# Transposing the attention weights by a DMA through memory instead of on TensorE in a top-k attention and MLP kernel

## The chip, the core and the metric

The kernel runs on one core of a Trainium2 chip. The core has five engines that each work through their own queue of instructions in order: TensorE (PE; its weight loads are listed as PEld), VectorE (DVE), ScalarE (ACT), GpSimd (POOL) and SyncE (SP), which here only issues DMAs. The metric is the device time of one execution in microseconds (us), the median of some runs. All times come from these runs or from one profiled execution.

## The reference

The first half is attention with the 32 largest scores of each row kept; the second is a two-layer network on its output. Cut to what is computed:

```python
# q, k, v: (8, 8, 576, 64) float32
scores = matmul(q, k.transpose(0, 1, 3, 2)) / sqrt(64)
kth = np.partition(scores, -32, axis=-1)[..., -32:-31]
scores = np.where(scores >= kth, scores, -1e9)
attn = np.exp(scores - scores.max(-1, keepdims=True))
attn = attn / (attn.sum(-1, keepdims=True) + 1e-9)
x = matmul(attn, v) -> (4608, 512)               # heads side by side
h = x @ w_in                                      # (512, 2048)
g = np.where(h >= 1, h, np.where(h <= -1, 0, (h + 1) ** 2 / 4))
out = g @ w_out                                   # (2048, 512)
```

Everything is float32.

## The kernel before

**Steps.** The attention is cut into 144 steps. A step takes 128 queries and two heads (or, for the last 64 rows of each head, two pairs of heads at once), so that its scores are two tiles of 128 x 576. In step m, `weights` (line 271) works on VectorE: four rounds of "the eight largest" (MAX8, line 283) and "strike them out" (line 292) on the pairwise maximum of a row's halves, then a correction from the pairwise minimum (lines 297 to 304), which gives the 32nd largest. ScalarE takes the exponentials (line 287) beside that. Line 312 keeps those whose score reaches the 32nd and sums them; lines 317 and 318 form the reciprocal of the sum; in most steps GpSimd multiplies the weights by it (line 325).

**Around a step.** `scores` (line 244) makes the scores two steps ahead on TensorE, and ScalarE copies them out of PSUM (line 261). `transpose_w` (line 333) follows a step later: eight TensorE transposes of 128 x 128 (line 344), and a ninth (line 352) for the two 64-column remainders, each into PSUM, and three ScalarE copies to SBUF (lines 345, 353). `values` (line 356) multiplies the transposed weights with v (line 364) and copies the result into `xT` (line 377), the input of the network. Once a tile of `xT` is complete, `mlp` (line 389) hands out units of work: `hidden` (four matmuls on line 394, the activation in pieces on ScalarE, lines 398 and 412, and on GpSimd, lines 413 to 415) and `final` (line 422, with one copy on line 426 and one store on line 428).

**Early and late.** In the first steps the weights of the network are also converted in 64 pieces by ScalarE, VectorE and GpSimd (`convert_piece`, line 110). While that goes on a step is "early", and its division is not done by GpSimd: ScalarE multiplies the identity by the reciprocals (line 322), and TensorE multiplies the weights by this diagonal, which transposes and divides in one (lines 342 and 349). The flag is `st["by_tensor"]`. 12 steps are of this kind and 132 are late ones. In late steps each piece of the network's weights is loaded once more and inspected by ScalarE (`inspect_piece`, line 138), one a step, until all 64 are through.

**The order of the work** is written out by hand for PE, DVE, ACT and POOL. The main loop goes through the steps; each has seven slots, and in each slot the next parts of `weights` are issued, then the other work due in that slot, and then `advance` adds units of the network by a rough count of times, as much as an equal share of the remaining work. In a late step before the change: values of step m - 2 and scores of step m + 2 at the start, the parts of `weights` as `[1, 2, 2, 2, 0, 0, 0]` (the last of the seven parts is the division), the transposes of step m - 1 in slot 2. As an engine works in order, what is issued behind a waiting instruction waits too. SP issues all DMAs in one queue.

The second call, `run(inner, False)`, is only executed if a test on the data asks for it; it is not executed with these inputs.

Of the kernel before, what the change touches and what calls it, by code (L numbers as in the profile page):

```python
# [10 lines left out]
F32 = mybir.dt.float32  # L11
U32 = mybir.dt.uint32
# [11 lines left out]
def kernel(  # L24
# [23 lines left out]
    SH = S // 2  # L48
    NK = DM // P
# [45 lines left out]
    def load(pool, i):  # L95
        if i < n_pieces and i not in loaded:
            if room and i < 28:
                loaded[i] = room[i % 8]
            else:
                loaded[i] = pool.tile([P, 2 * WC], U32, name="raw", bufs=3)  # L100
            nc.sync.dma_start(out=loaded[i], in_=pieces_of_weights[i][1].bitcast(U32))

    def words_of(pool, i):
        load(pool, i)
        words = loaded.pop(i).rearrange("p (n t) -> p n t", t=2)
        return words[:, :, 0], words[:, :, 1]
# [31 lines left out]
    def inspect_piece(pool, i):  # L138

        _, hi = words_of(pool, i)  # L140
        for x in range(2):
            sign = pool.tile([P, WC], F32, name="sign", bufs=3)
            nc.scalar.activation(sign, hi.bitcast(F32), AF.Sign, bias=tiny[:, x:x + 1],
                                 accum_out=signs[:, x, i:i + 1])


    def run(ctx, paired):
        xtp = ctx.enter_context(tc.tile_pool(name="xtp", bufs=3))
        stage = ctx.enter_context(tc.tile_pool(name="stage", bufs=2))
        att = ctx.enter_context(tc.tile_pool(name="att", bufs=2))  # L150
        ps = ctx.enter_context(tc.tile_pool(name="ps", bufs=1, space=PSUM))
# [119 lines left out]
        def weights(st, after):  # L271
# [47 lines left out]
            if st["by_tensor"]:  # L319
                st["rz"] = diag = att.tile([P, 2, P], F32, name="diag", bufs=1)  # L320
                for i in range(2):
                    nc.scalar.activation(diag[:, i, :], ident, AF.Copy, scale=rz[:, i:i + 1])
            else:
                for i in range(2):
                    nc.gpsimd.tensor_scalar(e[:, i, :], e[:, i, :], rz[:, i:i + 1], 1.0, ALU.mult, ALU.mult)  # L325
# [7 lines left out]
        def transpose_w(st):  # L333
            w = st["e"]
            st["wT"] = wT = att.tile([P, 2, NT, P], F32, name="wT", bufs=1)
            st["wTt"] = wTt = att.tile([P, P], F32, name="wTt", bufs=1)
            for i in range(2):
                pt = ps.tile([P, NT, P], F32, name="pw", tag="a", bufs=4)
                for c in range(NT):
                    w_in_place = w[:, i, main(i)][:, c * P:(c + 1) * P]  # L340
                    if st["by_tensor"]:
                        nc.tensor.matmul(pt[:, c, :], w_in_place, st["rz"][:, i, :], start=True, stop=True)
                    else:
                        nc.tensor.transpose(pt[:, c, :], w_in_place, ident)  # L344
                nc.scalar.copy(wT[:, i], pt)  # L345
            pt = ps.tile([P, P], F32, name="pwt", tag="a", bufs=4)
            if st["by_tensor"]:
                for i in range(2):
                    nc.tensor.matmul(pt[i * TL:(i + 1) * TL, :], w[:, i, tail(i)], st["rz"][:, i, :],
                                     start=True, stop=True)  # L350
            else:
                nc.tensor.transpose(pt, w.rearrange("p i n -> p (i n)")[:, SM:SM + P], ident)
            nc.scalar.copy(wTt, pt)


        def values(st):
            t, hp, v_in, v_tl = st["t"], st["hp"], st["keys"]["v"], st["keys"]["v_tl"]
            wT, wTt = st["wT"], st["wTt"]
            po = ps.tile([P, P], F32, name="po", tag="ph", bufs=3)
            if t < NT:  # L360
                for c in range(NT + 1):
                    for j in range(2):
                        h = 2 * hp + j
                        nc.tensor.matmul(po[j * D:(j + 1) * D], v_in[:, h, c, :] if c < NT else v_tl[0][:, h, :],  # L364
                                         wT[:, j, c, :] if c < NT else wTt, start=(c == 0), stop=(c == NT))
            else:
                for i in range(2):
                    cols = slice(i * TL, (i + 1) * TL)
                    for c in range(NT + 1):
                        for j in range(2):  # L370
                            h = 2 * (hp + i) + j
                            nc.tensor.matmul(po[j * D:(j + 1) * D, cols], v_in[:, h, c, :] if c < NT else v_tl[1][:, h, :],
                                             wT[:, i, c, j * TL:(j + 1) * TL] if c < NT else wTt[:, j * TL:(j + 1) * TL],
                                             start=(c == 0), stop=(c == NT))
            xT, col = st["xT"]
            if t < NT:
                nc.scalar.copy(xT[:, hp, col:col + P], po)  # L377
            else:
                nc.scalar.copy(xT[:, hp:hp + 2, col:col + TL], po.rearrange("p (i n) -> p i n", i=2))
# [88 lines left out]
        mlp_pool = ctx.enter_context(tc.tile_pool(name="mlp", bufs=1))  # L468
        pending = deque()
# [5 lines left out]
        def convert(time):  # L475

            nonlocal converted, begun
            while begun < min(converted + (2 if paired else 1), n_pieces):
                pipe.append(convert_piece(mlp_pool, begun, not paired))
                next(pipe[-1])  # L480
                begun += 1
# [3 lines left out]
            for i in range(begun, converted + 6):  # L485
                if i < converted + (2 if paired else 3) + (begun > converted) or room and i < 28:
                    load(mlp_pool, i)

        def inspect():
            nonlocal inspected  # L490
            room.clear()
            if paired and inspected < n_pieces:
                inspect_piece(mlp_pool, inspected)
                inspected += 1
                load(mlp_pool, inspected)
# [3 lines left out]
        pe_time, dve_time, done, scored, usable = 9.0, 12.0, {}, {}, {0: 0.0}  # L499
# [70 lines left out]
        for i in range(2):  # L570
            load(mlp_pool, i)
        next(first)
        for i in range(2, 8 if room else 3):
            load(mlp_pool, i)
# [12 lines left out]
        def values_until(m):  # L587
            nonlocal valued, pe_time
            while valued < min(m, n):
                pe_time = max(pe_time, transposed + 1.8) + 1.25  # L590
# [13 lines left out]

        for m in range(n + 2):
            early = converted < n_pieces
            coming = min((r + 2 - m for r in ready if r + 2 > m), default=1)
            if not early:
                values_until(m - 1)
                begin_at(m + 2)  # L610
            share = min((total - spent) / (n + 2 - m), sum(work[0] for work in pending) / coming)
            top_k, parts = None, [0] * SLOTS
            if m < n:
                top_k = weights(state[m], state[m + 1] if m + 1 < n else None)
                parts = [1] * SLOTS if early else [1, 2, 2, 2, 0, 0, 0]
# [5 lines left out]
            for slot in range(SLOTS):  # L621
# [6 lines left out]
                elif slot == 3:  # L628
                    inspect()
                if slot == 1 + (not early) and 1 <= m <= n:  # L630
                    pe_time = max(pe_time, done[m - 1] + 2.0) + 1.0
                    transpose_w(state[m - 1])
                    transposed = pe_time
                if slot == 2 and m == n and paired:
                    judge(ps, att)
                if slot == 2 and early:
# [3 lines left out]
                if slot == 4 and early:  # L640
                    begin_at(m + 2)
                if slot == (5 if early else 4):
# [63 lines left out]
```

## Time and profile before

| | |
|---|---|
| median of 3 runs | 1746.18 us (1745.42 to 1746.61) |
| the profiled execution | 1746.35 us |
| its span, first to last instruction | 1744.5 us |
| granted TensorE clock, mean | 0.982 of full speed |
| late steps | 132, from about 190 to 1700 us |
| DMA, mean over the span | 43 GB/s |

A group of instructions in the profile is one line, engine and operation, written out<-in with the names of the tiles; it shows the number of instructions, their total busy time and mean length, and the idle time of the engine just before them with what ended it. A table of windows gives each engine's busy time in stretches of the span. A chain of waits follows the work that ended last back to the start. Lengths of matmuls are those of a pipeline: successive ones overlap.

### The profile page before, as it was taken

The numbers are of one execution on the slowest core, as the hardware profiler recorded it, in microseconds if no ns is written. First come the engines' busy times: TensorE is split into PE (matmuls) and PEld (weight loads), VectorE is DVE, ScalarE is ACT, GpSimd is POOL, SyncE is SP. The second block draws the span as 40 slices with busy tenths as digits, with TensorE's granted clock in tenths as the row PEclk, the third lists the DMA queues.
The fourth block names the chain that finished last, engine by engine and source line by source line (L and its number), as shares of the span: only waits on it lengthen the run. The fifth ranks groups of instructions, "written<-read, shape, count | busy, mean of one in ns | idle before, by whom it ended". The sixth has DMA issues, their size and how long they took to land.

```text
span 1744.5 us, 33535 instructions
## 1 busy us (share of the span) xinstructions
PE 1639.4 (94%) x10665; PEld 1151.5 (66%) x10665; DVE 1537.0 (88%) x4875; ACT 1083.2 (62%) x2942; POOL 946.9 (54%) x1668
## 2 busy tenths in 40 slices
PE   5588989999999999999999999999999999999998
PEld 4476575667766757476756767567667666666665
DVE  7999979888899999999987999999997998899752
ACT  6688575676667857576655647556555555466452
POOL 5689183665544817264646645436365554555550
PEclk7799999999999999999999999999999999999999
DMA  8333112111121112111200101000010000000000
GB/s 253 116 98 97 46 30 65 44 43 41 42 63 52 44 49 65 46 49 41 62 13 22 25 22 44 17 24 17 23 39 19 19 10 14 13 7 7 7 7 15
DMA packets 116668, 74.63 MB, mean 43 GB/s; under 512 B 87296, under 2 KB 95488, under 8 KB 116480
## 3 DMA queue, kind: packets, MB, share of 16 engines
q1 hardware_dynamic: 116480, 72.37, 14.5%
q8 instruction: 87, 1.43, 0.3%
q14 instruction: 101, 0.83, 0.2%
HBM read 62.91 MB, written 9.44 MB: 41 GB/s over the span
## 4 chain that ended last, share of the span: by engine, by line
PE 65%; DVE 14%; POOL 11%; ACT 6%; issue 3%; DMA 0%; POOLq 0%; DVEq 0%; SPq 0%; ACTq 0%
PE py L422 25%; PE ph L394 18%; PE sp L258 7%; PE po L364 7%; PE pw L344 5%; DVE tops L283 4%; DVE more L292 3%; POOL g L415 3%; POOL r L414 3%; DVE e L312 3%; POOL e L325 2%; POOL r L413 2%; ACT s L261 1%; DVE seconds L300 1%; ACT r L398 1%
## 5 line engine op out<-in xcount | busy, mean ns | idle before, releaser
L394 PE MATMUL ph<-xT,w_in 128*128 128x128 f32 (+1 forms) x3200 | 558.0, 326 | 14.4 <-ACT g L412 13.2
L422 PE MATMUL py<-w_out,g 128*128 128x512 f32 x1152 | 530.9, 600 | 2.0 <-ACT y L426 2.0
L394 PEld LDWEIGHTS ph<-xT,w_in 128*128 128x128 f32 x3200 | 472.3, 192 | 87.9 <-ACT g L412 26.0
L325 POOL TENSOR_SCALAR e<-e,rz 128x576 f32<-128x576 f32 x264 | 195.0, 750 | 520.2 <-DVE rz L318 488.8
L283 DVE MAX8 tops<-more 128x8 f32<-128x288 f32 x1152 | 465.4, 445 | 0.0
L292 DVE MATCH_REPLACE8 more<-tops,more 128x288 f32<-128x288 f32 x864 | 375.6, 442 | 0.0
L422 PEld LDWEIGHTS py<-w_out,g 128*128 128x128 f32 x1152 | 205.2, 190 | 224.1 <-issue 215.8
L312 DVE SCALAR_TENSOR_TENSOR e<-s,kth,e 128x576 f32<-128x576 f32 x288 | 245.7, 881 | 116.6 <-ACT e L287 116.3
L398 ACT ACTIVATE r<-ph,half 128x128 f32<-128x128 f32 (+1 forms) x400 | 166.5, 416 | 216.8 <-POOL g L415 156.7
L415 POOL TENSOR_TENSOR g<-r,g 128x128 f32<-128x128 f32 (+1 forms) x384 | 255.9, 666 | 30.2
L413 POOL TENSOR_SCALAR r<-r 128x128 f32<-128x128 f32 (+1 forms) x368 | 173.2, 471 | 132.0 <-ACT r L398 131.7
L414 POOL TENSOR_TENSOR r<-r 128x128 f32<-128x128 f32 (+1 forms) x368 | 213.9, 581 | 30.7
L261 ACT ACTIVATE s<-sp 128x288 f32<-128x288 f32 x576 | 195.2, 421 | 56.8 <-PE sp L258 36.8
L287 ACT ACTIVATE e<-s,nmax 128x576 f32<-128x576 f32 x288 | 213.4, 770 | 7.7
L364 PEld LDWEIGHTS po<-wT,v_in 128*64 128x64 f32 x2048 | 111.8, 137 | 87.9 <-issue 53.2
L258 PE MATMUL sp<-kT,qT 64*128 64x288 f32 x1024 | 163.9, 437 | 4.2 <-ACT kT L218 2.3
L364 PE MATMUL po<-wT,v_in 128*64 128x128 f32 x2048 | 145.5, 280 | 18.7 <-ACT g L412 11.3
L345 ACT COPY wT<-pw 128x512 f32<-128x512 f32 x288 | 154.0, 589 | 13.1 <-PE pw L344 10.6
L344 PEld LDWEIGHTS pw<-ident,e 128*128 128x128 f32 x1056 | 122.2, 142 | 60.0 <-issue 24.4
L344 PE MATMUL pw<-ident,e 128*128 128x128 f32 x1056 | 141.0, 276 | 16.2 <-ACT s L261 10.4
L377 ACT COPY xT<-po 128x128 f32<-128x128 f32 x128 | 34.1, 266 | 195.8 <-PE po L364 195.5
L412 ACT ACTIVATE g<-ph,minus 128x128 f32<-128x128 f32 (+1 forms) x368 | 153.6, 417 | 0.0
(91 smaller groups left out, 1595.1 us busy)
## 6 DMA issues: line engine op xcount, KB each, us to landing
raw<-in_moe_w_out_dram SPq DMA_DIRECT2D x64, 256.0 KB, 2.6
raw<-in_moe_w_in_dram SPq DMA_DIRECT2D x36, 256.0 KB, 2.7
k_in<-in_k_dram SPq DMA_DIRECT2D x64, 128.0 KB, 2.9
q_in<-in_q_dram SPq DMA_DIRECT2D x32, 256.0 KB, 3.1
v_in<-in_v_dram SPq DMA_DIRECT2D x8, 1024.0 KB, 5.8
out_dram<-y SPq DMA_DIRECT2D x32, 256.0 KB, 2.3
kT<-in_moe_w_in_dram SPq DMA_DIRECT2D x16, 256.0 KB, 4.0
v_in<-in_moe_w_in_dram SPq DMA_DIRECT2D x12, 256.0 KB, 4.5
```

The lines of the kernel that those rows point to most:

```text
L258: nc.tensor.matmul(o[:, a0 - c0:a1 - c0], qT[d, g, :], kT[d, g, k0:k0 + a1 - a0], start=True, stop=True)
L283: nc.vector.max(out=tops[:, i, r:r + 8], in_=src[:, i, :])
L287: nc.scalar.activation(e[:, i, :], s[:, i, :], AF.Exp, bias=nmax[:, i:i + 1])
L292: nc.vector.match_replace(out=rest[:, i, :], in_to_replace=tops[:, i, r:r + 8], in_values=src[:, i, :], imm_value=LOWEST)
L312: nc.vector.scalar_tensor_tensor(out=e[:, i, :], in0=s[:, i, :], scalar=last[:, i:i + 1], in1=e[:, i, :], op0=ALU.is_ge, op1=ALU.mult, acc ...
L325: nc.gpsimd.tensor_scalar(e[:, i, :], e[:, i, :], rz[:, i:i + 1], 1.0, ALU.mult, ALU.mult)
L344: nc.tensor.transpose(pt[:, c, :], w_in_place, ident)
L364: nc.tensor.matmul(po[j * D:(j + 1) * D], v_in[:, h, c, :] if c < NT else v_tl[0][:, h, :], wT[:, j, c, :] if c < NT else wTt, start=(c == ...
L394: nc.tensor.matmul(ph, w_in[:, kk, f * P:(f + 1) * P], xT[:, kk, c0:c1], start=(kk == 0), stop=(kk == NK - 1))
L414: nc.gpsimd.tensor_tensor(out=r, in0=r, in1=r, op=ALU.mult)
L415: nc.gpsimd.tensor_tensor(out=g, in0=r, in1=g, op=ALU.add)
L422: nc.tensor.matmul(py, gs[f][:, i * P:(i + 1) * P], w_out[:, f, :], start=(f == 0), stop=(f == NF - 1))
```

## The change

Late steps no longer transpose on TensorE. A new function, `move_w`, splits each 32-bit weight into its two 16-bit halves with ScalarE copies (the low halves of a row side by side, then the high ones), stores them to a tile in memory, and loads that tile with a transposing DMA, which works on 16-bit elements. In the loaded tile the two halves of a weight lie side by side again, so that it can be read as float32. The tile has nine blocks of 128 (`BLOCKS`), the middle one holding both remainders, in the place of the former `wT` and `wTt`. `transpose_w` is left for early steps, in the diagonal form alone.

The order of a late step changes too. The division is not issued in slot 3 but as the last part of the step, behind the network's work of slots 4 to 6. `move_w` stands in slot 1. Scores of step m + 2 and values of step m - 2 go from the start of a step to slot 4. The rough count of times has the transposed weights ready 13.0 us after the step's end instead of 1.8 us after the transposes.

The buffers of the conversion are now in a pool of their own (`words`), which is closed once the conversion is over; its room is used for a new pool (`late`) with two buffers for the transposed weights, one for the halves, and two instead of three for the pieces under inspection. The first late step is a step of passage in which neither is done.

```diff
+        dram = ctx.enter_context(tc.tile_pool(name="dram", bufs=3, space=bass.MemoryType.DRAM))
...
         def transpose_w(st):
             w = st["e"]
-            st["wT"] = wT = att.tile([P, 2, NT, P], F32, name="wT", bufs=1)
-            st["wTt"] = wTt = att.tile([P, P], F32, name="wTt", bufs=1)
+            st["wT"] = wT = words.tile([P, BLOCKS, P], F32, name="wT")
...
+        def move_w(st):
+            st["wT"] = wT = late.tile([P, BLOCKS, P], F32, name="wT", bufs=2)
+            halves = late.tile([P, 2, 2 * S], U16, name="halves")
+            for i in range(2):
+                nc.scalar.copy(halves[:, :, i * S:(i + 1) * S], st["e"][:, i, :].bitcast(U16).rearrange("p (k t) -> p t k", t=2))
+            rows = dram.tile([P, 2, 2 * S], U16, name="rows")
+            nc.sync.dma_start(out=rows, in_=halves)
+            nc.sync.dma_start_transpose(wT.bitcast(U16), rows.rearrange("p t k -> (p t) k"))
+
+        def block(i, c):
+            return i * (NT + 1) + c if c < NT else NT
...
-                pe_time = max(pe_time, transposed + 1.8) + 1.25
+                pe_time = max(pe_time, ready_at[valued]) + 1.25
                 values(state[valued])
...
+        first_late = None
         for m in range(n + 2):
             early = converted < n_pieces
...
-            if not early:
-                values_until(m - 1)
-                begin_at(m + 2)
+            if not early and first_late is None:
+                first_late = m
+            elif not early and late is None:
+                conversion.close()
+                late = ctx.enter_context(tc.tile_pool(name="late", bufs=1))
...
-                parts = [1] * SLOTS if early else [1, 2, 2, 2, 0, 0, 0]
+                parts = [1] * SLOTS if early else [1, 2, 2, 1, 0, 0, 0]
...
-                elif slot == 3:
+                elif slot == 3 and late is not None:
                     inspect()
-                if slot == 1 + (not early) and 1 <= m <= n:
-                    pe_time = max(pe_time, done[m - 1] + 2.0) + 1.0
-                    transpose_w(state[m - 1])
-                    transposed = pe_time
+                if slot == 1 and 1 <= m <= n:
+                    if state[m - 1]["by_tensor"]:
+                        pe_time = max(pe_time, done[m - 1] + 2.0) + 1.0
+                        transpose_w(state[m - 1])
+                        ready_at[m - 1] = pe_time + 1.8
+                    else:
+                        move_w(state[m - 1])
+                        ready_at[m - 1] = done[m - 1] + 13.0
...
-                if slot == 2 and early:
+                if slot == 2 and (early or m == first_late):
                     values_until(m)
...
-                if slot == 4 and early:
+                if slot == 4:
                     begin_at(m + 2)
+                    if not early:
+                        values_until(m - 1)
```

## The prediction

> **What bounds the kernel now.** I read the busy times and the chain that ended last first, then the busy times in 100 us windows, then the groups of instructions of the lines that the change touches, the waits, the timeline of a few late steps and of the end, and the DMA issues. From the page, the busy times and the chain's shares:
>
> ```profile
> PE 1639.4 (94%) x10665; PEld 1151.5 (66%) x10665; DVE 1537.0 (88%) x4875; ACT 1083.2 (62%) x2942; POOL 946.9 (54%) x1668
> ...
> PE 65%; DVE 14%; POOL 11%; ACT 6%; issue 3%; DMA 0%; POOLq 0%; DVEq 0%; SPq 0%; ACTq 0%
> ```
>
> Two engines are nearly full: TensorE carries most of the chain, and VectorE is only 6 points behind it. So freeing TensorE can be worth only the distance to VectorE, and that distance differs by stretch. In the table of windows (stretch, its length, busy time and instructions of PE, PEld, DVE, ACT, POOL, then clock, DMA share, GB/s):
>
> ```profile
> 300.00:400.00 100.00, 93.03 (x656) 67.33 (x655) 84.05 (x273) 69.07 (x204) 56.16 (x120) 1.00 0.15 42
> ...
> 500.00:600.00 100.00, 95.50 (x658) 72.87 (x659) 97.39 (x310) 76.22 (x217) 62.41 (x112) 1.00 0.16 45
> 600.00:700.00 100.00, 97.44 (x642) 66.23 (x641) 97.39 (x311) 67.63 (x186) 50.36 (x82) 1.00 0.19 55
> ...
> 1300.00:1400.00 100.00, 98.36 (x613) 69.56 (x612) 82.72 (x264) 58.67 (x154) 51.68 (x98) 0.98 0.08 19
> ```
>
> The reader is to see two kinds of stretch. In 500 to 900 and 1100 to 1200 (call it A) VectorE is busy 95 to 98%: both engines bound. In the rest of 190 to 1700 (call it B) TensorE is at 93 to 100% and VectorE at 69 to 93%: TensorE bounds. Counting the reciprocals of line 318, one per step, A holds 46 steps in 500 us (10.9 us each) and B 86 steps in 1010 us (11.7 us each). The 132 late steps are just those whose transposes are on line 344 (1056 matmuls, 8 a step).
>
> **What goes.** The groups of the lines concerned (busy time, mean ns of one | idle before):
>
> ```profile
> L325 POOL TENSOR_SCALAR e<-e,rz 128x576 f32<-128x576 f32 x264 | 195.0, 750 | 520.2 <-DVE rz L318 488.8
> ...
> L287 ACT ACTIVATE e<-s,nmax 128x576 f32<-128x576 f32 x288 | 213.4, 770 | 7.7
> ...
> L345 ACT COPY wT<-pw 128x512 f32<-128x512 f32 x288 | 154.0, 589 | 13.1 <-PE pw L344 10.6
> L344 PEld LDWEIGHTS pw<-ident,e 128*128 128x128 f32 x1056 | 122.2, 142 | 60.0 <-issue 24.4
> L344 PE MATMUL pw<-ident,e 128*128 128x128 f32 x1056 | 141.0, 276 | 16.2 <-ACT s L261 10.4
> ```
>
> *TensorE.* The mean of 276 ns is a length, not an interval: matmuls overlap. In the timeline at 1000.09 us eight transposes take 1.04 us, and the first matmul after the ninth (line 352) starts at 1001.08 after line 344 began at 999.99: 1.09 us for all nine. 132 steps x 1.09 = 144 us of TensorE. Its waits for the scaled weights (23 us of the two line 344 rows on line 325, 12 us on line 414) go as well, but the wait on the new transfer stands in their place, so I count neither.
>
> *A:* TensorE would give 46 x 1.09 = 50 us, but VectorE is busy 97.4 + 97.4 + 97.5 + 95.4 + 97.3 = 485 of the 500 us, so at most 15 are to be had. I take 12. *B:* TensorE gives 86 x 1.09 = 94 us, 1010 to 916. VectorE's work there (1341 us in 200 to 1700, less A's 485, plus some 9 in 190 to 200) is 865 us, still under 916, so the gain is whole: 94. Together -106 us.
>
> **What comes, beside other work.** *ScalarE* loses two copies of 589 ns and one of 288 (1.47 us) and gains two splits of 1152 16-bit elements. No row has that shape. Below: the slope of the plain copies, 421 ns at 288 elements to 589 at 512, is 0.75 ns an element, so 0.589 + 640 x 0.75 = 1.07 us; above: twice the 576-element row of line 287, 1.54 us. I take 1.3, nearer to the middle as the operand lies in SBUF like that of line 287 but needs no exponential. Net 2.6 - 1.47 = +1.1 us a step (0.7 to 1.6), 149 us in all: ScalarE from 1083 to 1232 us, 75% of 1650. Priced at nothing, hidden behind the other two engines; without that cover it costs up to its 149 us. What is queued behind a split is the next step's work of slots 1 to 4: relu and shift of the MLP (lines 398, 412), which frees one of three PSUM tiles for TensorE, and the evacuation of scores (line 261). The splits wait for line 325 of the step before. ScalarE reaches them only after the new step's first MAX8 (0.9), nmax (0.2), both exponentials (1.5) and one or two MLP pairs (0.9 each), some 3.5 us into the step; GpSimd's scaling is done 1.5 us after the reciprocal unless MLP work stands before it. So mostly no stall.
>
> *GpSimd* keeps its work; the division moves behind the MLP work of slots 4 to 6. It now idles 488.8 us at line 325 for the reciprocal with MLP work queued behind (ScalarE waits 156.7 us on line 415). That may give some us; it also makes the scaled weights up to one MLP unit later (0.6 + 1.0 + 0.7 us). Bounded by -10 and +10 us, I take 0.
>
> *VectorE* keeps all its instructions. The scores move from a step's start to slot 4; they are still issued more than a step before VectorE needs them, so nothing.
>
> *SP and the DMA rings.* Each late step adds a store of 128 x 1152 x 4 bytes = 576 KB and a transposing load of as much, on SP, the second waiting for the first to land. Behind the waiting SP stand the weights to inspect, keys, queries and output, each issued a step or more ahead. What stands before it (output after line 426, keys after line 218) waits on ScalarE or TensorE work that precedes the splits anyway. The rows to go by (KB, us from issue to landing):
>
> ```profile
> q_in<-in_q_dram SPq DMA_DIRECT2D x32, 256.0 KB, 3.1
> v_in<-in_v_dram SPq DMA_DIRECT2D x8, 1024.0 KB, 5.8
> out_dram<-y SPq DMA_DIRECT2D x32, 256.0 KB, 2.3
> ```
>
> From the two loads, 2.7 us per 768 KB: the store is 2.3 + 320 KB x 0.0035 = 3.4 us. The transposing load is nowhere in this trace. Below: as a plain load, 3.1 + 1.1 = 4.2 us. Above: 256 KB of 256-byte pieces took 3.1 us, 128 KB (k_in) 2.9; scaled without any overlap that is 7.0 and 13 us. I take 4.2, as it is one transfer of 576 KB like v_in's, and keep 13 as the far end. The chain is then 1.5 (scaling) + 2.6 + 3.4 + 4.2 = 11.7 us plus the 3.5 us in which ScalarE gets there, where the store's start is what matters: store 6 us into a step, landed transposed at 13.7, and the values are asked for in slot 4 of the next step, at about 10.7 + 6 = 16.7. Three us of slack, plus whatever TensorE lags.
>
> The Trainium skill speaks on both sides, and nothing in this trace can show which holds. "VectorE: DVE Perf Modes", section "The three transpose paths", gives a 128x128 16-bit transpose by DMA as 1309 ns against 390 on TensorE and advises TensorE where PSUM will do; 18 such blocks in series would be an estimated 23.6 us a step, twice a step's time, and the kernel some 3500 us. "DMA: Bandwidth & Descriptors", section "Latency and other measured facts", gives 261 GB/s for transposing DMAs; by that the load's data take 2.3 us and the forecast below stands.
>
> **At the end** no TensorE work is planned between the last division and the last values: today line 325 ends at 1696.4 and the last values start at 1699.2; now split 2.6, store 3.4 and load 4.2 follow, start 1706.6: +7.5 us. The exchange of the conversion buffers for the new ones waits once for old readers: +2.
>
> **Sum.** The profiled execution took 1746.35 us (span 1744.5, 1.85 around it), 0.2 from the median 1746.18, so no correction: 1746.35 - 106 + 7.5 + 2 = **1650 us**.
>
> **The rivals.**
> *VectorE becomes the only bound and everything else hides.* For it: A is there already. Against: in B TensorE still needs 916 against 865. Time: 1650 less B's 51 and A's 3 = 1596.
> *ScalarE eats half.* For it: VectorE already waits 116.3 us for its exponentials (line 312 on line 287) and it runs in order, so 1.3 us pieces delay scores, MLP and exponentials alike. Against: it idles 38%, mostly waiting for TensorE. At 0.5 us a step lost: 1650 + 66 = 1716.
> *The transposing load is slow (slower than before).* Place: SP's rings, where the next store queues behind the load. The period is then store + load, 3.4 + T; it equals today's 11.5 us a step (1510 / 132) at T = 8.1, and from there each us costs 132 us. At the far row, T = 13: 190 + 132 x 16.4 + 54 = 2409 us. For it: no row shows such a transfer, and 7 to 13 us is what small pieces would cost. Against: the rings are busy 4 to 20% now, and a load of 1024 KB lands in 5.8.
> *It does not do what it says:* if line 344's work stayed or its room stayed empty because of the new wait, no change, 1746. The code drops those matmuls, so only the wait could do that, with T near 8.
>
> **Chances.** Forecast (1615 to 1690) 0.55; VectorE the only bound (1590 to 1615) 0.08; ScalarE or the wait for the load eats half (1690 to 1742) 0.15; no change 0.03; slow load (from 1750 up without a useful end) 0.19. About 0.2% is what a measurement of this kernel can tell from no change. So faster 0.78, same 0.03, slower 0.19. The range runs from the VectorE bound, 1595, to 1755, which leaves out most of the slow load and a sliver below.
>
> **What would show it.** TensorE's busy time down by some 130 us or more and line 344 gone but for the diagonal form; VectorE 92% or more in every window; two ScalarE splits a step of 1.1 to 1.5 us; the store landing in about 3.4 us and the load in about 4.2; waits of line 364 on the load under 20 us in all. It is wrong if the load lands later than 8 us after its issue, if ScalarE's share passes 85%, or if SP stands at the load's issue for most of a step.

## The result and the profile after

The changed kernel took 1793.22 us (median of 4 runs, 1788.13 to 1796.52), the kernel before 1745.82 beside it: a ratio of 1.0268, 95% interval 1.0244 to 1.0293. The forecast was 1650: the change was to save 96 us and costs 47. The profiled execution has a span of 1794.7 us; the mean granted clock fell from 0.982 to 0.942.

From the page of the changed kernel, the busy times and the chain's shares:

```profile
PE 1564.4 (87%) x9477; PEld 1069.1 (60%) x9477; DVE 1561.5 (87%) x4875; ACT 1209.2 (67%) x2810; POOL 955.3 (53%) x1668
...
PE 49%; POOL 18%; ACT 16%; DVE 8%; DMA 4%; issue 4%; POOLq 0%; SPq 0%; ACTq 0%; DVEq 0%
```

1188 matmuls are gone, as meant. But no engine is full now, and the chain, two thirds TensorE before, has a third on GpSimd and ScalarE. The same stretches as in the prediction, by the windows of the changed kernel (columns as there):

```profile
500.00:600.00 100.00, 85.47 (x504) 62.29 (x504) 86.05 (x274) 72.13 (x174) 51.66 (x96) 0.88 0.52 136
600.00:700.00 100.00, 86.88 (x519) 56.32 (x518) 88.74 (x279) 68.64 (x161) 49.37 (x76) 0.95 0.52 137
...
1300.00:1400.00 100.00, 91.16 (x504) 61.02 (x504) 82.84 (x261) 66.33 (x149) 56.94 (x105) 0.95 0.44 121
```

VectorE was to be at 92% or more in every window. In these two, where it had been full at 97.4, it fell to 86 and 89: there the new kernel waits. Not everywhere: from 700 to 800 it is still at 96, from 1100 to 1200 at 97, and from 1000 to 1100 it rose from 92 to 97. The new work itself, from the groups and the DMA issues:

```profile
L328 POOL TENSOR_SCALAR e<-e,rz 128x576 f32<-128x576 f32 x264 | 220.7, 846 | 404.0 <-DVE rz L321 338.8
...
L356 ACT COPY halves<-e 128x1152 uint16<-128x1152 uint16 x264 | 291.6, 1146 | 92.6 <-POOL e L328 91.2
```

```profile
rows<-halves SPq DMA_DIRECT2D x132, 576.0 KB, 2.9
...
wT<-rows SPq DMA_TRANSPOSE x132, 4.7
```

A split takes 1.15 us (1.3 predicted), the store lands after 2.9 (3.4) and the transposing load after 4.7 (4.2). So the slow load is not what happened. What did, in the table of waits (engine, line waiting, line waited for: us in all, times, longest):

```profile
POOL r L422 <- ACT r L407: 275.8, 75, 17.9
...
DVE e L315 <- ACT e L290: 113.3, 52, 7.7
...
ACT s L264 <- PE sp L261: 104.4, 51, 5.4
ACT halves L356 <- POOL e L328: 91.2, 54, 3.1
...
PE po L373 <- DMA wT<-rows: 25.3, 9, 6.9
PEld po L373 <- DMA wT<-rows: 22.5, 12, 5.4
```

The same waits in the kernel before (its lines 413, 312 and 261 are 422, 315 and 264 now):

```profile
POOL r L413 <- ACT r L398: 131.7, 46, 10.0
DVE e L312 <- ACT e L287: 116.3, 80, 6.3
ACT s L261 <- PE sp L258: 36.8, 81, 1.7
```

GpSimd's wait for the relu has doubled and ScalarE's wait for the scores almost tripled; VectorE's wait for the exponentials, as a total, has not grown; line 356 is new. The two rows of TensorE on the transfer add up to 48 us at most.

I then counted in the trace by steps, from one reciprocal to the next, instead of by windows. "Late" is from the first reciprocal of the late part to the last, 131 steps; "tail" is from there to the end; a step is "VectorE-full" when VectorE is busy 95% or more of it; "half clock" is the time in late steps and tail at a granted clock of 0.5.

| | late | tail | half clock | VectorE-full: steps, mean | other: steps, mean, TensorE busy |
|---|---|---|---|---|---|
| before | 1506.7 | 52.7 | 16 | 79, 10.64 | 52, 12.82, 96% |
| after | 1530.4 | 80.3 | 162 | 91, 10.73 | 40, 13.86, 87% |

Of the 50 us between the two profiled executions 24 are in the late steps and 28 behind the last reciprocal. The first number is the riddle, since 106 were to be saved there. Taken apart on VectorE it is odd as well: VectorE stood for 153 us of the late steps before and stands for 150 now, but its own instructions, the same ones, grew from 1354 to 1380 us (more on this under 11).

### The profile page after: what moved, and what is told of

Same layout as the page of the kernel before. It is cut to its first block, busy times and chain, and to the rows that moved or that the text cites. A ratio compares the mean times of both kernels' runs of the same rounds, so it can differ in the third digit from the quotient of the medians.

```text
span 1794.7 us, 31008 instructions
## 1 busy us (share of the span) xinstructions
PE 1564.4 (87%) x9477; PEld 1069.1 (60%) x9477; DVE 1561.5 (87%) x4875; ACT 1209.2 (67%) x2810; POOL 955.3 (53%) x1668
## 4 chain that ended last, share of the span: by engine, by line
PE 49%; POOL 18%; ACT 16%; DVE 8%; DMA 4%; issue 4%; POOLq 0%; SPq 0%; ACTq 0%; DVEq 0%
PE py L431 24%; PE ph L403 11%; POOL g L424 6%; PE po L373 6%; PE sp L261 5%; POOL r L423 5%; ACT halves L356 5%; POOL e L328 4%; DMA wT<-rows 3%; POOL r L422 3%; ACT r L407 2%; DVE tops L286 2%; DVE more L295 2%; ACT g L421 2%; DVE e L315 2%
## 5 line engine op out<-in xcount | busy, mean ns | idle before, releaser
L403 PEld LDWEIGHTS ph<-xT,w_in 128*128 128x128 f32 x3200 | 494.2, 199 | 123.8 <-ACT g L421 58.1
L328 POOL TENSOR_SCALAR e<-e,rz 128x576 f32<-128x576 f32 x264 | 220.7, 846 | 404.0 <-DVE rz L321 338.8
L431 PEld LDWEIGHTS py<-w_out,g 128*128 128x128 f32 x1152 | 214.9, 193 | 261.0 <-issue 223.0
L315 DVE SCALAR_TENSOR_TENSOR e<-s,kth,e 128x576 f32<-128x576 f32 x288 | 262.0, 940 | 114.5 <-ACT e L290 113.3
L356 ACT COPY halves<-e 128x1152 uint16<-128x1152 uint16 x264 | 291.6, 1146 | 92.6 <-POOL e L328 91.2
L422 POOL TENSOR_SCALAR r<-r 128x128 f32<-128x128 f32 (+1 forms) x368 | 152.2, 414 | 276.2 <-ACT r L407 275.8
L373 PE MATMUL po<-wT,v_in 128*64 128x128 f32 x2048 | 153.9, 291 | 38.0 <-DMA wT<-rows 25.3
L261 PEld LDWEIGHTS sp<-kT,qT 64*128 64x128 f32 x1024 | 94.8, 196 | 82.5 <-issue 46.5
L303 DVE MAX8 seconds<-more 128x8 f32<-128x288 f32 x288 | 118.3, 452 | 14.0
L300 DVE TENSOR_TENSOR more<-s 128x576 f32<-128x576 f32 x144 | 117.5, 816 | 4.5
```

Of the source, the lines that this page charges most:

```text
L261: nc.tensor.matmul(o[:, a0 - c0:a1 - c0], qT[d, g, :], kT[d, g, k0:k0 + a1 - a0], start=True, stop=True)
L315: nc.vector.scalar_tensor_tensor(out=e[:, i, :], in0=s[:, i, :], scalar=last[:, i:i + 1], in1=e[:, i, :], op0=ALU.is_ge, op1=ALU.mult, acc ...
L356: nc.scalar.copy(halves[:, :, i * S:(i + 1) * S], st["e"][:, i, :].bitcast(U16).rearrange("p (k t) -> p t k", t=2))
L403: nc.tensor.matmul(ph, w_in[:, kk, f * P:(f + 1) * P], xT[:, kk, c0:c1], start=(kk == 0), stop=(kk == NK - 1))
L431: nc.tensor.matmul(py, gs[f][:, i * P:(i + 1) * P], w_out[:, f, :], start=(f == 0), stop=(f == NF - 1))
```

## The experiments

Each was timed beside the kernel before on one chip (medians of the kernel before 1745.1 to 1746.8); ratios are to that kernel, with the 95% interval. Edits are against the changed kernel unless another is named.

**1. Only the new order, transposes back on TensorE** (a1). `move_w` in late steps is replaced by `transpose_w` with TensorE's nine transposes, in slot 1 (the transposes themselves are not shown here).

```diff
-                        move_w(state[m - 1])
-                        ready_at[m - 1] = done[m - 1] + 13.0
+                        pe_time = max(pe_time, done[m - 1] + 2.0) + 1.0
+                        transpose_w(state[m - 1])
+                        ready_at[m - 1] = pe_time + 1.8
```

> The changed kernel with TensorE transposes in its late steps again (nine a step, three ScalarE copies), but in the new order: division last in a step, transposes in slot 1, scores and values in slot 4. Theory ORDER (the moved instructions make the loss): slower than before by 1.5% or more, some 1775 to 1800 us. Theory SPLIT (ScalarE's splits and their wait for GpSimd) and theory LANDING (TensorE waits for the load and its granted clock falls): about as before, 1735 to 1755 us, TensorE's clock about 0.98.

Measured: 2021.72 us, ratio 1.1587 [1.1568, 1.1607]. Slower, as theory ORDER said, but far above its 1800. TensorE itself now stands at the late division:

```profile
DVE e L315 <- ACT e L290: 276.7, 104, 8.3
...
PEld pw L346 <- POOL e L328: 250.8, 109, 5.4
...
PE pw L346 <- POOL e L328: 212.5, 81, 5.2
```

So transposes on TensorE do not go with a late division, and this run does not give the order's price within the new form.

**2. The division early again** (a2).

```diff
-                parts = [1] * SLOTS if early else [1, 2, 2, 1, 0, 0, 0]
+                parts = [1] * SLOTS if early else [1, 2, 2, 2, 0, 0, 0]
```

> The changed kernel with the division in slot 3 again, the parts as [1, 2, 2, 2, 0, 0, 0]. ORDER: 15 us or more faster than the changed kernel's 1793. SPLIT: the splits' wait for the scaled weights (91 us in all) shrinks, 10 to 30 us faster, but GpSimd stands at the reciprocal longer with the network's work behind it. LANDING: within 10 us of 1793.

Measured: 1741.07 us, ratio 0.9992 [0.9976, 1.0007]. One digit takes 52 us off the changed kernel. By steps: late 1472.6, tail 76.8. The whole rest of the change is thus a gain of 34 us in the late steps and a loss of 24 in the tail, in a profiled execution that is 5 us below the median of the ten.

**3. Splits cut to almost nothing** (a3).

```diff
-            halves = late.tile([P, 2, 2 * S], U16, name="halves")
+            halves = fixed[0]
...
-                nc.scalar.copy(halves[:, :, i * S:(i + 1) * S], st["e"][:, i, :].bitcast(U16).rearrange("p (k t) -> p t k", t=2))
+                nc.scalar.copy(halves[:, :, i * S:i * S + 2], st["e"][:, i, 0:2].bitcast(U16).rearrange("p (k t) -> p t k", t=2))
```

> The changed kernel with the splits cut to two weights of each row (the rest of the halves is a constant, so the values are not the attention's): ScalarE loses some 2 us a step, the store still waits for the scaled weights, both DMAs stay whole. SPLIT: most of the loss goes, 1700 us or less. LANDING: the chain to the landing is 2 us shorter, so some waits go: 1760 to 1785. ORDER: 1770 or more.

Measured: 1736.61 us, 0.9948 [0.9932, 0.9965], 57 below the changed kernel. No theory had said this; the splits cost on their own.

**4. Nobody waits for the transfer** (a4).

```diff
-            st["wT"] = wT = late.tile([P, BLOCKS, P], F32, name="wT", bufs=2)
+            wT = late.tile([P, BLOCKS, P], F32, name="wT")
+            st["wT"] = fixed[0]
```

> The changed kernel with the late values multiplied by a constant tile instead of the loaded one (so the output is not the attention's): splits, store and transposing load stay, only nobody waits for the landing. LANDING: TensorE's stretched matmuls and half of its new idle time go, granted clock back to 0.97 or more, 1720 us or less. SPLIT: 1770 or more, since the splits still hold up the activations. ORDER: 1770 or more.

Measured: 1779.18 us, 1.0196 [1.0177, 1.0215], only 14 below. The wait for the landing, though plain in the table, is a small part.

**5. The end of the program** (b1, against a2). Behind the last reciprocal of the changed kernel, from its timeline (start us, us, engine, line; idle before and its releaser):

```profile
1730.64 1.47 POOL L328 TENSOR_SCALAR e<-e,rz 128x576 f32<-128x576 f32 x2
1731.42 2.20 ACT L356 COPY halves<-e 128x1152 uint16<-128x1152 uint16 x2 [2.65 <-POOL e L328]
...
1734.71 0.34 SPq L358 DMA_DIRECT2D rows<-halves  x1
...
1737.67 2.57 SPq L359 DMA_TRANSPOSE wT<-rows  x1
...
1742.50 1.97 PE L373 MATMUL po<-wT,v_in 128*64 128x128 f32 x16 [6.91 <-DMA wT<-rows]
...
1744.83 1.22 PE L431 MATMUL py<-w_out,g 128*128 128x512 f32 x1
```

The last reciprocal was at 1714.5. GpSimd had 16 us of network pieces before the division, TensorE stood 6.91 us for the load, and the network's finals, which needed none of this, stood behind it. The edit lets all pending units go first:

```diff
                 if slot == 4:
                     begin_at(m + 2)
+                    if m == n + 1:
+                        while pending:
+                            advance(8.0, 0.0, True)
                     if not early:
                         values_until(m - 1)
```

> The variant with the division in slot 3 (a2_division_early, 1741 us), in which all of the network's waiting work is issued before the last step's values instead of behind them. Theory TAIL (some 20 us of the loss lie behind the last step: TensorE stands at the last load with 32 matmuls of 430 ns ready but queued behind it): the time from the last reciprocal to the end falls from 77 to about 60 us, total 1720 to 1728. If the tail is long for another reason (halved clock, slower last chunk): 1735 or more.

Measured: 1730.28 us, 0.9911 [0.9886, 0.9935], 11 below a2; tail 76.8 to 63.2.

**6. The early division without splits** (b2: the edits of 2 and 3 together).

> a2_division_early with the splits cut to two weights of each row (the values are not the attention's). Theory LOOP (with the division last, GpSimd ends its step's network work, then scales, then waits while ScalarE splits before it activates again; so a split's time is paid in steps that GpSimd bounds, and only with the division last): within 12 us of a2's 1741. Theory SPLIT (ScalarE's 2.3 us a step are paid wherever the division stands): 1700 us or less.

Measured: 1705.2 us, 0.9773 [0.9757, 0.9789]; 36 below a2. By steps: late 1445.5, tail 74.6. So the splits cost some 36 us with the division early, and 57 with it last. Without them the transfer can also start earlier, but that is little of it: TensorE's two rows on the transfer add up to 38.9 us here against 48.8 in a2, and to 45.8 in a3 against 47.8 in the changed kernel.

**7. GpSimd's load taken down in both forms** (b3: the kernel before, b4: a2; the square of a hidden unit is left out in late steps).

```diff
-                    nc.gpsimd.tensor_tensor(out=r, in0=r, in1=r, op=ALU.mult)
+                    if converted < n_pieces:
+                        nc.gpsimd.tensor_tensor(out=r, in0=r, in1=r, op=ALU.mult)
```

> The kernel before without GpSimd's squaring on line 414 in late steps (so the network's activation is another one). Theory GPSIMD (45 of the late steps are bounded by GpSimd, 104 us above VectorE's floor of 10.2 us a step, and nothing that frees TensorE shortens them): most of the squaring's time in those steps comes back, 1660 to 1700 us. Theory TENSORE (TensorE bounds everywhere but in the two stretches of full VectorE): 1735 or more.

> a2_division_early without GpSimd's squaring in late steps, as in b3_before_no_square. GPSIMD: the DMA form now gains against b3 what it did not gain with GpSimd full, 40 us or more below b3, some 1640 us. TENSORE: as far from b3 as a2 is from the kernel before, within 15 us of it.

Measured: b3 1696.78 us, 0.9724 [0.9708, 0.9741]; b4 1675.19, 0.9592 [0.9576, 0.9608]. The kernel before gains 48 us by a lighter GpSimd with every TensorE instruction left in. TensorE was not the only bound; the gap between the forms grows from 4 to 22 us, neither of the two figures expected. How much of that is real is open: in the profiled executions the late steps of the two forms differ by 34 us with the full GpSimd and by 35 with the lighter one.

**8. TensorE's time put back** (c1, against a2; then d1, against c2). c1 puts them into a PSUM tile of the shared ring, ahead of the values.

```diff
+                if not state[valued]["by_tensor"]:
+                    idle = ps.tile([P, NT, P], F32, name="idle", tag="a", bufs=4)
+                    for i in range(9):
+                        nc.tensor.transpose(idle[:, i % NT, :], ident, ident)
```

> a2_division_early with nine TensorE transposes that nobody reads just before the late values, so that TensorE has again the matmuls that the change took away. Theory FREED (what a2 gains in its steps, 34 us, it gains by TensorE's free time): 20 to 40 us slower than a2's 1741. Theory CLOCK (95 us at half the granted clock eat what was freed; matmuls in the gaps keep it up): the time at half clock falls under 40 us and the total is within 10 us of a2 or below.

Measured: 1937.84 us, 1.1087 [1.1069, 1.1106]. The run answers nothing, as the new transposes stand in a wait of their own: at their line the weight loads waited 196.2 us for ScalarE to copy the scores out of PSUM (line 264). d1 writes them into the values' own tile instead:

```diff
+            if not st["by_tensor"]:
+                for i in range(9):
+                    nc.tensor.transpose(po, ident, ident)
```

> c2_split_later with nine TensorE transposes written into the values' own PSUM tile just before the values overwrite it, so that nobody waits for a tile more than without them (in c1_nine_more they waited 126 us for a PSUM tile). Theory FREED (the gain of the DMA form is TensorE's freed time): back by 20 us or more, 1736 to 1760 us. Theory CLOCK (the gaps and the halved clock had eaten most of what was freed): within 10 us of c2's 1716.

Measured: 1763.36 us, 1.0101 [1.0084, 1.0118], 47 above c2. Half-clock time falls from 52 to 14 us and the mean clock rises from 0.972 to 0.982. Having this TensorE work removed is worth 47 in this order, net of what the clock gives back and of TensorE's standing for the transfer, which the added work fills (its two rows fall from 44.6 to 19.8 us). In the late steps, 46 us longer, nearly all of it appears as VectorE's wait for the exponentials, in c2 and then in d1:

```profile
DVE e L315 <- ACT e L290: 65.2, 33, 6.1
```

```profile
DVE e L315 <- ACT e L290: 108.1, 53, 8.1
```

**9. Where the splits and the scores stand** (c2, c3: against b1).

```diff
-                if slot == 1 and 1 <= m <= n:
+                if 1 <= m <= n and slot in (1, 2) and slot == (1 if state[m - 1]["by_tensor"] else 2):
```

> b1_drain_first with splits, store and load a slot later (2 instead of 1), so that a unit of activations stands ahead of the splits in ScalarE's queue. Theory QUEUE (the splits cost 36 us by standing before activations and scores in ScalarE's queue): 5 to 20 us faster than b1's 1730, unless the landing, then some 2 us later, makes TensorE wait at the values. Theory LENGTH (they cost by their length, wherever they stand): within 5 us of b1.

Measured: 1715.98 us, 0.983 [0.9813, 0.9846], the fastest version that does all the work: 30 us below the kernel before and 14 below b1.

c3 issues the scores of step m + 2 at a step's start again, as before the change.

```diff
+            if late is not None:
+                begin_at(m + 2)
...
-                    begin_at(m + 2)
+                    if late is None:
+                        begin_at(m + 2)
```

> b1_drain_first with the scores of step m + 2 at the start of a late step, as before the change, instead of in slot 4. Theory ORDER OF SCORES (ScalarE stands 101 us at the scores of a2 against 37 in the kernel before, with the next exponentials behind): 10 to 30 us faster than b1's 1730. If the place of the scores is of no account: within 6 us of b1.

Measured: 1776.77 us, 1.0176 [1.0136, 1.0215], 46 above b1. The move of the scores to slot 4 is worth about as much here as the whole of TensorE's freed time (47 in d1).

**10. One slot later still** (d2, against c2: the edit of c2 with slot 3 in the place of 2).

> c2_split_later with splits, store and load in slot 3. Theory QUEUE: a few us faster again, 1705 to 1713, until the landing is late. LANDING: the chain of 2.3 + 2.9 + 4.7 us is now issued some 3 us later than in b1, TensorE waits for it at line 373 by 40 us or more in all, 1720 or slower.

Measured: 1746.77 us, 1.0006 [0.9988, 1.0023], 31 above c2. TensorE's wait for the landing rose by some 12 us, VectorE's wait for the exponentials by 27. Slot 2 lies between two losses; why slot 3 costs so much is not settled.

**11. Why a late division costs** (d3, then e1 and e2). d3 is the changed kernel with the edit of c2.

> The changed kernel (division last) with splits, store and load in slot 2. Theory LOOP (the division last costs 52 us because ScalarE comes to the splits before GpSimd has scaled, and both stand): the wait of the splits for GpSimd falls from 91 to under 40 us and the total from 1793 to 1755 or less. If the division's place costs by itself (scaling behind the network's work, whoever waits): 1775 or more.

Measured: 1784.96 us, 1.0229 [1.0198, 1.0259], only 8 lower. ScalarE's wait for the division fell to 54 us, GpSimd's wait for the hidden units hardly. e1 cuts the bond between the two queues and leaves GpSimd's order alone; e2 is the same cut with the division early. Both leave the weights undivided, and both have one buffer instead of two for the inspected signs, which makes room for the tile `spare`.

```diff
-                    nc.gpsimd.tensor_scalar(e[:, i, :], e[:, i, :], rz[:, i:i + 1], 1.0, ALU.mult, ALU.mult)
+                    nc.gpsimd.tensor_scalar(spare[0] if spare else e[:, i, :], e[:, i, :], rz[:, i:i + 1], 1.0, ALU.mult, ALU.mult)
```

> The changed kernel with the division still last in a step, but in late steps GpSimd writes its product to a tile that nobody reads, and the splits read the undivided weights: so the values are those of undivided weights. GpSimd has the same instructions in the same order, and ScalarE's splits no longer wait for them. RING (the division's late place costs because ScalarE, with its whole queue, stands at the split until GpSimd has divided, and GpSimd stands before the division until ScalarE has done a hidden unit): the time falls to that of the early division, 1735 to 1755 us, and GpSimd's wait for the hidden units (line 422 on 407, 256 us from 188 to 1690) falls to near 100. PLACE (what costs is GpSimd's division among the network's pieces by itself, whoever reads it): 1775 to 1795, and that wait stays above 200.

> The kernel of the early division with the same edit: GpSimd's product goes to a tile that nobody reads, and the splits read the undivided weights, whose values are used. In that kernel ScalarE hardly waited for the division, so both theories expect it within 10 us of 1741; it is here so that the tile and the edit have a price of their own.

Measured: e1 1742.04 us, 0.9984 [0.9973, 0.9996]; e2 1744.18, 0.9999 [0.9989, 1.0009]. e2 is 3 us above a2, within the intervals of the two, so the tile and the buffer cost little. With nobody reading the product, a division last costs nothing in total. From the waits of e1:

```profile
POOL spare L328 <- DVE rz L321: 361.7, 48, 11.6
...
POOL r L424 <- ACT r L409: 208.8, 53, 15.1
...
DVE e L315 <- ACT e L290: 59.3, 33, 6.1
...
PE po L375 <- DMA wT<-rows: 24.2, 9, 4.8
...
PEld po L375 <- DMA wT<-rows: 22.7, 9, 5.2
```

The time is what the ring theory said; GpSimd's own wait is not (near 100 was expected, and above 200 was a sign of the other theory). GpSimd may stand 209 us, as long as ScalarE doesn't stand for it: VectorE's wait for the exponentials, which ScalarE makes, is about half of the 113.3 of the changed kernel. An earlier transfer is not the reason: TensorE's two rows on it add up to 46.9 us here and 47.8 there.

The late place has a price of its own all the same. VectorE's instructions in the late steps take 1380 us in the changed kernel and 1383 in e1, but 1362 in a2 and 1364 in e2; line 315 has a mean of 0.95 us in e1 and 0.91 in e2, and GpSimd's line 328 one of 0.84 and 0.76. A late division can fall beside VectorE's longer instructions, and then both take longer: the two of line 328 that begin at 315.58 in the changed kernel, beside line 300, take 2.08 us, and those at 1730.64, after VectorE's last step, 1.47. In e1 VectorE stands 19 us less than in e2 (96 and 115), which makes up for it.

## Why the prediction was wrong, step by step

**The prices were right.** Split, store and load were within 0.5 us of what was measured, SP was not blocked for a step (it holds the load's issue 2.6 us in the median, 2.2 at least and 6.9 at most), and the rival of the slow load is false. The prediction had tied a slower kernel to that rival alone, and its three signs of being wrong did not come either: the load landed later than 8 us in only 1 of 132 cases, ScalarE is at 67%, and SP did not stand at the load's issue for most of a step. TensorE's wait for the load, foreseen under 20 us in all, is up to 48. TensorE's nine transposes were a little overpriced: from the first matmul of line 344 to the one behind the ninth it is 0.98 us (median of the 132 steps), not 1.09, so some 130 us in all and not 144. The start at 999.99 is not in the timeline, where the first matmul is at 1000.09.

Of the two pages of the Trainium skill weighed there, "DMA: Bandwidth & Descriptors", section "Latency and other measured facts", comes near: by its 261 GB/s the data take an estimated 2.3 us, and in the trace the packets of a load take 2.8 us (median of the 69 loads that had no other packets of their size beside them), which is 211 GB/s. The serial estimate of 23.6 us a step from "VectorE: DVE Perf Modes", section "The three transpose paths", does not hold for this one large DMA: the whole load took 4.7.

**B: "the gain is whole: 94", with A's 12.** This step failed first. It took TensorE as the bound in windows of 100 us because VectorE stood at 69 to 93% there. But a window mixes steps of two kinds. Two stretches of the kernel before, one with four hidden units and one with finals only (columns as above):

```profile
593.40:604.80 11.40, 11.40 (x75) 9.31 (x75) 11.13 (x34) 9.40 (x26) 10.32 (x15) 1.00 0.19 48
625.10:635.30 10.20, 10.20 (x61) 5.83 (x58) 9.93 (x34) 6.37 (x17) 1.63 (x3) 1.00 0.23 70
```

Both are full of TensorE and of VectorE at once; in the first GpSimd is busy 91% as well, and VectorE's same 34 instructions take 1.2 us longer. Counted by steps, 79 of the 131 were VectorE-full already (mean 10.64 us), and TensorE work taken out of them hardly shortens them: in a2 the mean of such steps is 10.65. In the other 52 VectorE idled 129 us, and in the full ones 23. That sum alone would have allowed the 106, but it is not spread like the savings: a step can give back at most its 1.09 us of transposes, or VectorE's idle time if that is less. Added up over the 131 steps of the kernel before, this estimate is 77 us, and it could have been made from the trace of before. I also sorted what the steps took above 10.17 us, the shortest kind: 104 us lie in 45 steps with GpSimd 80% busy or more, and 49 in 42 further steps with TensorE at 97% or more. The experiments stay under the 77: without splits 61 us come off the late steps (b2), with splits 34 (a2), and between d1 and c2 it is 47; b3 got 48 from GpSimd alone. So in the place of 106 the sum should have had some 47 to 61 for TensorE, with the splits as a cost beside it.

**The division last: "Bounded by -10 and +10 us, I take 0."** It costs 52 (a2). The prediction let the scaling be done 1.5 us after the reciprocal "unless MLP work stands before it". In the kernel before it began 0.2 us after the reciprocal (median; one in ten later than 3.2). In the changed kernel that is 3.3, one in ten later than 12.3. What the runs point to is a ring of two queues in order: GpSimd reaches the division only behind a hidden unit, whose relu ScalarE makes (line 407); ScalarE reaches that relu only behind the split, which waits for the division of the step before (line 328). From the timeline of the changed kernel:

```profile
309.92 0.17 DVE L321 RECIPROCAL rz<-z 128x2 f32<-128x2 f32 x1
...
313.83 0.37 ACT L407 ACTIVATE r<-ph,half 128x128 f32<-128x128 f32 x1 [0.31 <-PE ph L403]
...
314.29 0.29 POOL L422 TENSOR_SCALAR r<-r 128x128 f32<-128x128 f32 x1 [12.58 <-ACT r L407]
...
315.58 2.08 POOL L328 TENSOR_SCALAR e<-e,rz 128x576 f32<-128x576 f32 x2
```

The reciprocal was there at 310.1, GpSimd was idle, and the division began at 315.58, behind a relu of 313.83. That is GpSimd's half of the ring; here the relu itself had last waited for TensorE (line 403), not for a split. ScalarE's half is the 91.2 us of line 356 on line 328. e1 shows that the cost hangs on ScalarE's wait for the division: with that bond gone the 51 us are gone, though GpSimd still stands 209 us. That the two halves close into a ring is argued, as GpSimd's wait did not fall as far as the ring theory said. And it stays open why d3, which took away 40% of ScalarE's wait, gained 8 us and not 20, although the same edit gained 14 with the division early (c2).

**"Priced at nothing, hidden behind the other two engines."** The splits cost 36 us (b2 against a2), 57 with the late division (a3). ScalarE is busy 67%, but everything passes through its one queue in order: scores, exponentials, relu, evacuations. The rival "ScalarE eats half" had the right mechanism, 0.5 us a step; measured are 36 / 132 = 0.27, and 0.43 with the late division, for the splits alone, without what the dropped copies gave back. To leave it out of the sum because of a share of busy time was the mistake.

**At the end: "+7.5 us".** It was +27.6, and +24 with the division early (a2). The sum followed the chain of one step and left out what stood before it on GpSimd (16 us of network pieces) and behind it on TensorE (the finals). b1 took 14 of that back in a2's kernel by order alone.

**The scores to slot 4: "so nothing".** The move is worth 46 us in the new form (c3), in the kernel's favour. In c3 TensorE waits 82.9 us for the transfer (values and scores stand apart there) and VectorE 138.3 for the exponentials, against 43.9 and 80.0 in b1 (TensorE's two rows added up); both grew, and which of them carries the 46 was not separated.

**The clock** was in no step. TensorE waiting for the load shows it in the windows of the changed kernel:

```profile
760.00:765.00 5.00, 0.11 (x2) 0.11 (x4) 4.93 (x22) 3.55 (x5) 1.63 (x3) 0.73 0.85 147
765.00:770.00 5.00, 5.00 (x32) 3.91 (x32) 4.79 (x13) 3.76 (x12) 0.00 (x0) 0.58 0.51 173
770.00:775.00 5.00, 0.62 (x6) 0.28 (x6) 4.93 (x20) 3.38 (x5) 1.62 (x3) 0.76 0.79 168
775.00:780.00 5.00, 5.00 (x31) 4.32 (x30) 4.79 (x15) 3.46 (x11) 0.00 (x0) 0.56 0.51 175
```

In gaps of 4.95 and 4.38 us the clock falls to half and stays there for some us behind them, and sixteen matmuls of the values that took 1.09 us at 757.4 take 1.98. TensorE's busy time fell by 75 us and not by the 130 of the transposes; the 146 us more at half clock can make up to 73 of busy time, so they can cover what is missing. "TensorE: Matmul & The Clock Gate", section "What's actually happening", of the Trainium skill says that an idle window of some 3.4 us halves the clock. In the trace it falls sooner: 2.4 and 2.2 us into these two gaps, and of the 31 stretches at half clock in the late steps of the changed kernel 26 began after less than 3.4 us without a matmul. In the 3.41 us before each of the 31 TensorE had been idle for 53% or more. The clock alone has no price from these runs. That it is not the main cause is argued from d1, which raises the clock of c2 and is slower, since its TensorE time counts more than the clock it wins.

Together, by the medians: the change without splits and with the division early is 40 us below the kernel before (b2: by the profiled executions 61 off the late steps, 22 more in the tail); the splits add 36 (a2), and the division's place adds 52. That is the 47 us between the two kernels, to within 1 us. The sum had -106 for the late steps, +9.5 for the tail and the exchange of buffers, and nothing for the splits and the division's place.

## What to carry to other kernels

Count the bound step by step, not in windows: when two engines are full in most steps, work taken from one of them is worth only the idle time of the other in the rest. A total of idle time over a window is too kind, as a step gives back no more than was taken out of it. Work added to an engine through whose queue everything passes in order can cost a part of its length even at 67% busy, and where two such queues wait for each other's pieces, the place of one instruction in a step can cost more than the whole change brings. When a transfer replaces an engine's work, go through the last step by itself, with what stands before and behind it on each queue.

## What the runs showed of the hardware

VectorE and GpSimd lengthen each other's instructions. In the two stretches of the kernel before, the first with GpSimd busy 91%, VectorE's line 269 took 1.05 against 0.74 us and line 312 2.04 against 1.56 for the same instructions, both with two inputs in SBUF; line 317, a one-input addition, took 0.56 against 0.17; MAX8 of line 283 was the same (3.23 and 3.22). It can also hit the other engine: line 297, of the same form as 269, took 0.76 in both, and the GpSimd instruction beside it took 0.95 where the same one took 0.40 at 595.31:

```profile
598.99 0.76 DVE L297 TENSOR_TENSOR more<-s 128x576 f32<-128x576 f32 x1
599.06 0.95 POOL L413 TENSOR_SCALAR r<-r 128x256 f32<-128x256 f32 x1
```

"GPSIMD Engine Reference", section "1. Specifications", of the Trainium skill says that the two engines contend when VectorE has two SBUF inputs or runs in a two-port mode; lines 269, 297, 312 and 283 fit that, and whether line 317 runs in such a mode the trace does not show. In b3, with 228 us less of GpSimd work, VectorE's busy time in the late steps fell from 1354 to 1326 us without any change to it.

A transposing load of 576 KB from memory lands 4.7 us after its issue (median) and holds SP for 2.6 us of that (2.2 to 6.9); the store of as much lands in 2.9. In the changed kernel the clock falls to half in stretches of 3.41 us or a multiple, 162 us in the late steps and the tail, most of them behind less than 3.4 us without a matmul (26 of the 31 in the late steps).
